# The last four chunks of one tile in seven products instead of eight, two loads on GpSimd's queue, and a start cut finer on TensorE

## Chip, cores, metric

The kernel runs on one core of a Trainium2 chip. Time is the device time of that core in microseconds (us). The engines are TensorE (PE, matrix products, with its weight loads PEld), VectorE (DVE), ScalarE (ACT), GpSimd (POOL) and SyncE (SP), which here only issues DMAs. An engine works through its own queue in order. A DMA is issued by an engine's queue and then moved by 16 DMA engines that all queues share.

## What is computed

Lightning attention in blocks with a decay for each head, and behind it a SwiGLU network. Cut to what matters (B = 4, H = 8, S = 768, D = 64; 3072 tokens, model dimension 512, inner dimension 1536):

```
for each block b of 64 positions:
    intra = (qb @ kb.T * Dmask) @ vb                  # Dmask: lam ** (i - j) for i >= j
    inter = (qb * lam_pow) @ kv_state
    out[b] = intra + inter
    kv_state = lam ** 64 * kv_state + (kb * rev_pow).T @ vb
x = out, heads side by side                           # 3072 x 512
g = x @ w_gate; v = x @ w_val                         # 512 x 1536 each
result = (g * sigmoid(g) * v) @ w_out                 # 1536 x 512
```

## The kernel before

**Tiles and groups.** The tokens are handled in six tiles t = 0..5 of 512 tokens. A tile is made of two groups of 256 tokens; group g (0 to 11) belongs to tile g // 2. For each group k, q and v are loaded (load_group, L263; load_fp32, L109), k is cast to bfloat16 by ScalarE and q scaled and cast by VectorE (cast_scaled, L277, its two instructions at L281 and L283), both are transposed by one DMA (dma_transpose, L268, tile qkt), and v is scaled by GpSimd into v_s (v_scale, L255). From group 6 on k and q are loaded in four DMAs each (L122), of 64 partitions and 128 KB.

**Attention of a group** has these pieces on TensorE: scores(g) (L376), masked by VectorE into ssb (L381); core_a(g), the product with the state (inter, L502); core_b(g), the product within the block (intra, L515), whose result ScalarE copies into the tile's input xt (evac, L527); upd_mm(g) (L408), the update of the state, copied out by ScalarE (upd_copy, L430) and added up by GpSimd (state, L463); the copies of the state for TensorE (kvn, L443, L445) stand in a list kvq and are issued by kv_flush. attend(g) (L863) runs core_a(g), then upd_mm, scores of g + 1, core_b(g) and state of g + 1.

**The network, two ways.** In tiles 0 to 3 each of the twelve chunks of 128 inner columns is a step: ffn_fc (L580) makes four gate products of 512 columns (L558), silu on ScalarE (L562), four value products (L574) and the multiplication into h on VectorE (L577). In tiles 4 and 5 ffn_unit(t, j) (L686) makes four chunks at once, 2j, 2j + 1 and the same of the second half, by a seven-product scheme: the model dimension and the inner dimension are each cut in two, and the tokens of a tile are split by blocks, so that a product of two 2 x 2 block matrices takes seven block products and not eight. Each of the seven is eight instructions of 256 columns at L703 (two matrices, two chunk columns, two parts of the model dimension). For it sums and differences of weights are made on VectorE (w_combo, L651, instruction L666: n = 0, 1, 2 into ws, n = 3 in place into the weights), and of the inputs (x_combo, L672, instruction L684; the fourth, n = 3, in place into xt). The unit copies and adds partial results with ScalarE (L737, L740) and VectorE (L745, L753), takes silu at L730 and multiplies at L733, three times on VectorE and once on GpSimd. The product with w_out is done in the same seven-product way in all tiles but tile 0 (out_units, L775, instruction L793), with combinations of w_out (wo_combo, L614) and of h (h_combo, L625, instruction L640).

**What sets the order.** Everything is written by hand: the kernel runs under a manual schedule, so each engine's instructions stand in the order in which the program makes them. `steps` is the list of chunks, `plan` says with at(step, fn, ...) what follows a step, and the loop at L1151 works it off. Small VectorE instructions (h_combo, and later x_combo, w_combo) stand in the list `trickle`, from which drip(n) takes n at places between products. Masks wait in `later` until run_later. PSUM has eight banks, handed out in a ring by bank(); a unit takes six fixed ones. SBUF tiles come from pools with few buffers: raw (10) for loads and combinations, qkt (3) for transposed q and k, h (5), ups (4), sil (3).

**Around the change.** Tile 3 is the loop of L1114 for t = 3: twelve chunks in the order 0, 1, 6, 7, 2, 3, 8, 9, 4, 5, 10, 11 (L1115), attend(8) after the sixth and attend(9) after the eleventh (AT, L1113), cast_scaled(9) and load_group(10) after the first, cast_scaled(10) and load_group(11) after the seventh (L1120 to L1122). WS (L1099) says after which step each w_combo comes; the lists from L1178 on gives what is dripped in out_units(2) (L1184). k of group 11 is loaded on ScalarE's queue (KACT, L325), all else on SP's. The kernel begins with TensorE products on constants (L179 to L184) that compute nothing.

Of the kernel before, what the change touches and what calls it, by code (L numbers as in the profile page):

```python
# [37 lines left out]
def _body(ctx, tc, nc, q, k, v, lam, moe_w_gate, moe_w_val, moe_w_out, out):  # L38
# [140 lines left out]
    for n in range(30):  # L179
        r = slice(n % 2 * 64, n % 2 * 64 + 64)  # L180
        nc.tensor.matmul(b[r, 0:8], warm[r, 0:64], warm[r, 0:8], start=True, stop=True, skip_group_check=True)
    warm_up(2)
    nc.tensor.matmul(lam_ps[:, 0:H], ones[:, 0:128], lam_row, start=True, stop=True)
    warm_up(4)  # L184
# [78 lines left out]
    def load_group(g, parts="kqv"):  # L263
        for src, what in ((k, "kraw"), (q, "qraw"), (v, "v")):
            if what[0] in parts:
                load_fp32(g, nc.scalar if what == "kraw" and g in KACT else nc.sync, src, what)

# [57 lines left out]
    KACT = (11,)  # L325
# [344 lines left out]
    XS0 = 4  # L670

    def x_combo(t, n, g):  # L672

        xt = st[("xt", t)]
        g = slice(0, 2) if g is None else slice(g, g + 1)
        b11, b12 = xt[:, g, 0:KH, 0], xt[:, g, 0:KH, 1]
        b21, b22 = xt[:, g, KH:MC, 0], xt[:, g, KH:MC, 1]
        if t not in xs:
            pool, tag = (qkt_pool, "qkt") if t == XS0 else (raw_pool, "raw")  # L680
            xs[t] = pool.tile([128, 3, 2, KH, BLK], BF16, name="xs", tag=tag)
        x = [xs[t][:, m, g] for m in range(3)]
        o, i0, i1 = ((x[0], b12, b11), (x[1], b22, x[0]), (x[2], b21, x[1]), (b12, b22, b12))[n]
        nc.vector.tensor_tensor(out=o, in0=i0, in1=i1, op=ALU.subtract)  # L684

    def ffn_unit(t, j, bk, early=None, mid=None, dr=(0, 0, 2)):  # L686
# [51 lines left out]
        for i in range(2):  # L738
            product(i, E[i], wa(0, 1), xb(0, 1), True)
            nc.scalar.copy(out=es[i], in_=E[i])  # L740
# [28 lines left out]
        h_combo(t, j)  # L769
# [328 lines left out]
    outs = []  # L1098
    WS = [(x, n, i, 0, 3) for x, n, i in ((110, 0, 0), (112, 0, 1), (206, 1, 0), (210, 1, 1), (301, 2, 0), (303, 2, 1))] + [(308, 3, 0, 0, 2), (309, 3, 1, 0, 2)]  # L1099
    XC = 8  # L1100
    D0 = (0, 0, 3)
# [8 lines left out]
    A9 = 10  # L1110
    C11 = None
    sns = {0: s1a, 1: s1b + s2h}
    AT = {2: (7, 10), 3: (A8, A9)}  # L1113
    for t in range(2, 4):  # L1114
        order = [c for j in range(FC // 4) for c in (2 * j, 2 * j + 1, FH + 2 * j, FH + 2 * j + 1)]  # L1115
# [4 lines left out]
        for j, g in ((4 if t == 2 else 0, 2 * t + 3), (8 if t == 2 else 6, 2 * t + 4)):  # L1120
            at(sn[j], cast_scaled, g)
            at(sn[j], load_group, g + 1)  # L1122
            if g > 7:
                at(sn[1 + j], v_scale, g, nc.gpsimd, 0, H // 2)
                at(sn[(1 if t == 2 else 2) + j], v_scale, g, nc.gpsimd, H // 2, H)
        for i in range(2):
            at(sn[AT[t][i]], attend, 2 * t + 2 + i)
        if t == 2:
# [6 lines left out]
            at(sn[9], h_combo, t, (0, 2))  # L1135
        else:
            at(sn[7], h_combo, t, (0, 2))
        at(sn[11], h_combo, t, 2)
    sn = sns[3]
    if C11 is not None:  # L1140
        at(sn[C11], cast_scaled, 11)
    XM = (1, 1)
    W3L = ()
# [3 lines left out]
    if not XM[0]:  # L1147
        for n in (0, 3, 1, 2):
            at(sn[XC], x_combo, 4, n, 0)

    for n, (t, fc, b0, b1) in enumerate(steps):  # L1151
# [6 lines left out]
        todo = plan.get(n, [])  # L1158
        busy = [f for f, x in todo if f in (attend, ahead, cast_scaled, v_scale)]
        if not busy:  # L1160
            drip(2 if len(trickle) > 4 else 1)
        for fn, *a in [(f, *x) for f, x in todo]:
            if fn is out_units:
                drip(sum(x[0] <= a[0] for x in trickle))
            fn(*a)
            if fn in (attend, ahead):
                run_later(1)
    run_later(len(later))
# [15 lines left out]
    out_units(2, many=list(M2))  # L1184
# [11 lines left out]
    trickle[:0] = [soon(w_combo, i, 3, (2, 3)) for i in range(2)]  # L1196
    def early():
        fixed[:] = [s0, s1]
        scores(11)

# [56 lines left out]
```

## Time and profile before

| | |
|---|---|
| runs | 217.79, 217.82, 219.28 us; median 217.82 |
| the profiled execution | 218.1 us |
| its span, first to last instruction | 216.3 us |
| instructions in it | 6883 |
| TensorE clock granted | 1.000 (mean) |
| HBM read, written | 28.31 MB, 6.29 MB |
| DMA on queue q1 (SP) | 38.22 MB |
| DMA on queue q10 (ACT) | 1.11 MB |

A row of the timeline reads: start in us, length in us, engine (with q: its queue), line, operation, what is written and read, count; in brackets the idle time just before and what ended it. A row of the chain of waits reads: start, length, engine, tile, line, count. A row of the stretches reads: stretch, its length, and for PE, PEld, DVE, ACT and POOL the busy time and the instructions, then the granted clock, the DMA share and GB/s. Ends of TensorE instructions are modelled, and a few of its records are missing from the trace.

### The profile page before, as it was taken

To read this page: it belongs to the slowest core of one execution; us is meant where nothing else is said; L and a number is where in the kernel's file an instruction comes from. 1 tells how busy PE (TensorE), PEld (TensorE's weight loads), DVE (VectorE), ACT (ScalarE), POOL (GpSimd) and SP (SyncE) were. 2 spreads that over 40 slices of the span, in tenths; PEclk is the share of its full clock that TensorE was granted. 3 is DMA by queue.
4 is the path that set the end of the run, shared out by engine and by line. 5 is a ranking of instruction groups with operands and counts; after the bars stand their busy time and mean duration, and the time that the engine had idled before them with its cause. 6 is when DMAs were issued, how large, how long until landed. Compare 5 with 4: busy or idle time off the path is not lost.

```text
span 216.3 us, 6883 instructions
## 1 busy us (share of the span) xinstructions
PE 209.8 (97%) x2813; PEld 153.3 (71%) x2816; DVE 149.5 (69%) x267; ACT 129.1 (60%) x280; POOL 92.3 (43%) x126
## 2 busy tenths in 40 slices
PE   8899999999999999999999999999999999999994
PEld 4666455888887447666754545888888888888883
DVE  1774447576677989775478988886797379961760
ACT  5788577666545254638368478754872766636522
POOL 6684755818498240685962336510740022200200
PEclk9999999999999999999999999999999999999999
DMA  6999999999999878999678899481000500005014
GB/s 189 346 354 345 378 337 321 290 249 232 315 352 151 191 214 190 257 186 238 168 169 236 203 230 215 103 225 68 2 5 3 194 0 3 0 3 194 0 52 146
DMA packets 88320, 39.76 MB, mean 184 GB/s; under 512 B 57698, under 2 KB 83938, under 8 KB 88290
## 3 DMA queue, kind: packets, MB, share of 16 engines
q1 hardware_dynamic: 84978, 38.22, 64.9%
q10 hardware_dynamic: 3312, 1.11, 2.0%
q8 instruction: 22, 0.36, 0.7%
q14 instruction: 8, 0.07, 0.1%
HBM read 28.31 MB, written 6.29 MB: 160 GB/s over the span
## 4 chain that ended last, share of the span: by engine, by line
PE 73%; DVE 7%; DMA 6%; SPq 5%; ACT 3%; issue 2%; POOL 2%; POOLq 1%; DVEq 0%
PE bank L793 20%; PE bank L703 15%; PE bank L558 13%; PE bank L574 13%; DMA woraw<-in_moe_w_out_dram 4%; PE bank L593 4%; SPq L122 2%; DMA qraw<-in_q_dram 2%; SPq L247 2%; DVE ws L666 2%; DVE h L577 1%; PE bank L515 1%; PE bank L146 1%; DVE wt L623 1%; PE bank L502 1%
## 5 line engine op out<-in xcount | busy, mean ns | idle before, releaser
L577 DVE TENSOR_TENSOR h<-sil,bank 128x256 bf16<-128x256 bf16 (+1 forms) x67 | 34.8, 531 | 26.3 <-PE bank L574 18.0
L558 PE MATMUL bank<-xt,wg_sb 128*128 128x256 bf16 (+1 forms) x268 | 52.5, 319 | 0.0
L574 PE MATMUL bank<-xt,wv_sb 128*128 128x256 bf16 (+1 forms) x268 | 52.4, 319 | 0.0
L562 ACT ACTIVATE sil<-bank 128x256 bf16<-128x256 f32 (+1 forms) x67 | 31.7, 479 | 23.7 <-PE bank L558 16.8
L574 PEld LDWEIGHTS <-wv_sb 128*128 128x128 bf16 x268 | 26.0, 98 | 15.8 <-DVE wv_sb L988 0.5
L558 PEld LDWEIGHTS <-wg_sb 128*128 128x128 bf16 x268 | 25.2, 98 | 13.8 <-DVE xt L527 0.2
L258 POOL TENSOR_TENSOR v_s<-v,dec 128x512 bf16<-128x512 f32 (+1 forms) x18 | 24.1, 1356 | 24.0 <-DMA v<-in_v_dram 16.0
L733 POOL TENSOR_TENSOR h<-sil,es 128x512 bf16<-128x512 bf16 x6 | 7.0, 1163 | 50.0 <-ACT sil L730 50.0
L793 PEld LDWEIGHTS <-h 128*128 128x128 bf16 x240 | 23.3, 98 | 3.4 <-issue 0.3
L793 PE MATMUL bank<-wo_sb,h 128*128 128x256 bf16 x180 | 21.6, 273 | 0.1
L793 PEld LDWEIGHTS <-hs 128*128 128x128 bf16 x180 | 17.6, 98 | 2.9
L357 DVE TENSOR_TENSOR ssb<-bank,causal 128x512 bf16<-128x512 f32 x24 | 15.4, 681 | 1.8 <-PE bank L350 1.8
L745 DVE TENSOR_TENSOR bank<-bank,es 128x512 f32<-128x512 f32 x12 | 7.8, 693 | 11.4 <-PE bank L703 10.1
L703 PEld LDWEIGHTS <-ws 128*128 128x128 bf16 x144 | 13.8, 97 | 2.3 <-issue 0.2
L793 PE MATMUL bank<-wt,hs 128*128 128x256 bf16 x120 | 15.0, 272 | 0.0
L730 ACT ACTIVATE sil<-bank 128x512 bf16<-128x512 f32 x18 | 10.7, 596 | 7.0 <-POOL h L733 4.6
L463 POOL TENSOR_TENSOR kvf<-kvs,ups 128x256 f32<-128x256 f32 x8 | 6.5, 813 | 19.1 <-ACT ups L430 19.1
L733 DVE TENSOR_TENSOR h<-sil,bank 128x512 bf16<-128x512 bf16 x18 | 12.2, 682 | 1.4 <-ACT sil L730 1.4
L703 PE MATMUL bank<-xs,ws 128*128 128x256 bf16 x96 | 12.8, 272 | 0.0
L527 ACT CAST xt<-bank 128x512 bf16<-128x512 f32 x19 | 11.6, 658 | 2.0 <-PE bank L515 1.5
L463 POOL TENSOR_TENSOR kvf<-kvf,ups 128x256 f32<-128x256 f32 x16 | 12.2, 763 | 0.9
L703 PE MATMUL bank<-xt,wg_sb 128*128 128x256 bf16 x72 | 10.8, 273 | 0.2 <-ACT ups L430 0.2
(119 smaller groups left out, 361.3 us busy)
## 6 DMA issues: line engine op xcount, KB each, us to landing
out_dram<-osb SPq DMA_DIRECT2D x22, 256.0 KB, 2.1
v<-in_v_dram SPq DMA_DIRECT2D x18, 256.0 KB, 4.5
woraw<-in_moe_w_out_dram SPq DMA_DIRECT2D x6, 512.0 KB, 7.6
qraw<-in_q_dram SPq DMA_DIRECT2D x24, 128.0 KB, 3.2
wraw<-in_moe_w_gate_dram SPq DMA_DIRECT2D x5, 512.0 KB, 7.2
wraw<-in_moe_w_val_dram SPq DMA_DIRECT2D x5, 512.0 KB, 6.9
kraw<-in_k_dram SPq DMA_DIRECT2D x20, 128.0 KB, 3.1
kraw<-in_k_dram SPq DMA_DIRECT2D x4, 512.0 KB, 6.6
```

The source lines that it names most:

```text
L258: eng.tensor_tensor(out=st[("vs", g)][:, h0:h1], in0=st[("v", g)][:, h0:h1].rearrange("p h (s d) -> p h s d", s=2), in1=vfac(g, h0, h1), o ...
L357: nc.vector.tensor_tensor(out=ssb[:, h2, 2 * c:2 * c + 2].rearrange("p a s n -> p a (s n)"), in0=sp[(c, h2)].rearrange("p (a x) -> p a x", ...
L463: nc.gpsimd.tensor_tensor(out=o, in0=f, in1=u, op=ALU.add)
L527: fns[r](out=xt[:, g % 2, :, r].rearrange("p h (m s) -> p h s m", s=2) if g < NAT0 else xt[:, g % 2, :, :, r * M:r * M + M], in_=op[r].rea ...
L558: nc.tensor.matmul(gp[:, 0:N], wg_sb[:, mc, fs], xt[:, b0 // 2:b1 // 2, mc].rearrange("p g b n -> p g (b n)"), start=(mc == 0), stop=(mc = ...
L562: nc.scalar.activation(sil[:, 0:N], gp[:, 0:N], AF.Silu)
L574: nc.tensor.matmul(vp[:, 0:N], wv_sb[:, mc, fs], xt[:, b0 // 2:b1 // 2, mc].rearrange("p g b n -> p g (b n)"), start=(mc == 0), stop=(mc = ...
L577: nc.vector.tensor_tensor(out=h_sb[:, fc % FH, b0:b1].rearrange("p b n -> p (b n)"), in0=sil[:, 0:N], in1=vp[:, 0:N], op=ALU.mult)
L703: nc.tensor.matmul(o[:, fi * 256:fi * 256 + 256], lhs(i, c, 2 * j + fi), rhs(c), start=(start and fi == 0 and c == 0), stop=(c == KH - 1), ...
L730: nc.scalar.activation(sil[key], src, AF.Silu)
L733: eng.tensor_tensor(out=h_of(half, r), in0=v3(sil[half, r]), in1=v3(src), op=ALU.mult)
L793: nc.tensor.matmul(o, lhs(f), rhs(f), start=(start and f == 0), stop=(f == FH - 1), skip_group_check=True)
```

## The change

It does four things. (1) The last four chunks of tile 3 (4, 5, 10, 11) leave the loop and are made by ffn_unit(3, 2) in a new function unit3; core_a(9) stands inside that unit, and upd_mm(10), scores(10), core_b(9) and state(10) behind it. For this x_combo runs for tile 3 as well, after chunk steps 3, 4, 6 and 7, and its fourth result goes into a tile of its own (in all tiles) and not into xt, since eight chunks of tile 3 still read xt as it was; all w_combo n = 0, 1, 2 are done by the end of tile 2, n = 3 for the columns of these four chunks after steps 0 and 5 of tile 3, and for the others in two halves in out_units(2). out_units(2) gets its banks from the unit. (2) k of groups 10 and 11 is loaded by GpSimd's queue; before, by SP's and ScalarE's. (3) At the start 33 small products stand in place of 30, and 24 products of 128 columns in place of 6 of 512. (4) h_combo of tiles 4 and 5 does the columns of units 0 and 1 at once after unit 1, and four VectorE instructions are dripped earlier in the first unit of tile 4 (E0, D0). By the built programs TensorE has 5721 instructions and had 5631, VectorE as many as before, ScalarE loses four DMAs and gains seven other instructions, SP loses four DMAs.

```diff
-    for n in range(30):
+    for n in range(33):
...
-    warm_up(2)
+    warm_up(8, 128)
     nc.tensor.matmul(lam_ps[:, 0:H], ones[:, 0:128], lam_row, start=True, stop=True)
-    warm_up(4)
+    warm_up(16, 128)
...
-                load_fp32(g, nc.scalar if what == "kraw" and g in KACT else nc.sync, src, what)
+                load_fp32(g, nc.sync if what != "kraw" else KQ.get(g, nc.sync), src, what)
...
-    KACT = (11,)
+    MH = 0
+    KQ = {10: nc.gpsimd, 11: nc.gpsimd}
...
-            pool, tag = (qkt_pool, "qkt") if t == XS0 else (raw_pool, "raw")
-            xs[t] = pool.tile([128, 3, 2, KH, BLK], BF16, name="xs", tag=tag)
-        x = [xs[t][:, m, g] for m in range(3)]
-        o, i0, i1 = ((x[0], b12, b11), (x[1], b22, x[0]), (x[2], b21, x[1]), (b12, b22, b12))[n]
+            pool, tag = (raw_pool, "raw") if t == 5 else (qkt_pool, "qkt")
+            xs[t] = pool.tile([128, 4, 2, KH, BLK], BF16, name="xs", tag=tag)
+        x = [xs[t][:, m, g] for m in range(4)]
+        o, i0, i1 = ((x[0], b12, b11), (x[1], b22, x[0]), (x[2], b21, x[1]), (x[3], b22, b12))[n]
...
         for i in range(2):
-            product(i, E[i], wa(0, 1), xb(0, 1), True)
+            product(i, E[i], wa(0, 1), xsum(3), True)
...
-        h_combo(t, j)
+        if t == 3 or j != MH:
+            h_combo(t, (0, 2) if t > 3 and MH == 0 and j == 1 else j)
...
+    def unit3():
+        bk = [(ring[0] + i) % 8 for i in range(6)]
+        ring[0] += 6
+        assert primed[bk[4]] == primed[bk[5]] == 512
+        ffn_unit(3, 2, bk, lambda: (drip(EU[0]), kv_flush()), lambda: (drip(EU[1]), core_a(9)), DU)
+        upd_mm(10)
+        upd_copy(10)
+        scores(10)
+        late, later[:] = later[:], []
+        core_b(9)
+        later[:] = late
+        state(10)
+        st["bk2"] = [bk[n] for n in (4, 0, 2, 5, 1, 3)]
+
-    WS = [(x, n, i, 0, 3) for x, n, i in ((110, 0, 0), (112, 0, 1), (206, 1, 0), (210, 1, 1), (301, 2, 0), (303, 2, 1))] + [(308, 3, 0, 0, 2), (309, 3, 1, 0, 2)]
-    XC = 8
-    D0 = (0, 0, 3)
+    WS = [(x, n, i, 0, 3) for x, n, i in ((110, 0, 0), (111, 0, 1), (206, 1, 0), (207, 1, 1), (210, 2, 0), (211, 2, 1))] + [(300, 3, 0, 2, 3), (305, 3, 1, 2, 3)]
+    DU = (0, 0, 2)
+    XT = (3, 4, 6, 7)
+    EU = (0, 0)
+    E0 = 4
+    D0 = (0,0,0)
...
-    A9 = 10
...
-    AT = {2: (7, 10), 3: (A8, A9)}
+    AT = {2: (7, 10), 3: (A8,)}
     for t in range(2, 4):
-        order = [c for j in range(FC // 4) for c in (2 * j, 2 * j + 1, FH + 2 * j, FH + 2 * j + 1)]
+        order = [c for j in range(FC // 4 - 1) for c in (2 * j, 2 * j + 1, FH + 2 * j, FH + 2 * j + 1)]
...
-                at(sn[(1 if t == 2 else 2) + j], v_scale, g, nc.gpsimd, H // 2, H)
-        for i in range(2):
-            at(sn[AT[t][i]], attend, 2 * t + 2 + i)
+                at(sn[1 + j], v_scale, g, nc.gpsimd, H // 2, H)
+        for i, x in enumerate(AT[t]):
+            at(sn[x], attend, 2 * t + 2 + i)
...
             at(sn[9], h_combo, t, (0, 2))
+            at(sn[11], h_combo, t, 2)
         else:
             at(sn[7], h_combo, t, (0, 2))
-        at(sn[11], h_combo, t, 2)
+            for n, x in enumerate(XT):
+                at(sn[x], x_combo, 3, (0, 3, 1, 2)[n], None)
...
-    W3L = ()
+    W3L = (0, 1)
...
         todo = plan.get(n, [])
+        front = [x for x in todo if x[0] is w_combo or x[0] is x_combo]
+        todo = [x for x in todo if x not in front] + front
...
     run_later(len(later))
+    unit3()
+    run_later(len(later))
     new_xt(5)
...
-    out_units(2, many=list(M2))
+    out_units(2, bk=st["bk2"], many=list(M2))
...
-    trickle[:0] = [soon(w_combo, i, 3, (2, 3)) for i in range(2)]
     def early():
         fixed[:] = [s0, s1]
         scores(11)
+        drip(E0)
```

## The prediction

> **What bounds the kernel now.** I read the page first, then the busy time by stretches, the chain of waits, and last the timelines of single engines around tile 3, where most of the change lies.
>
> ```profile
> PE 209.8 (97%) x2813; PEld 153.3 (71%) x2816; DVE 149.5 (69%) x267; ACT 129.1 (60%) x280; POOL 92.3 (43%) x126
> ...
> PE 73%; DVE 7%; DMA 6%; SPq 5%; ACT 3%; issue 2%; POOL 2%; POOLq 1%; DVEq 0%
> ```
>
> TensorE (PE) is busy for 97% of the span and holds 73% of the chain. A busy PE need not be a fast PE, so the second view asks for the stretches one by one (columns: PE, PEld, DVE, ACT, POOL busy, clock, DMA share).
>
> ```profile
> 110.20:122.40 12.20, 12.20 (x63) 5.40 (x61) 10.99 (x14) 8.35 (x17) 5.54 (x5) 1.00 0.84 207
> 123.80:135.70 11.90, 11.90 (x178) 5.97 (x171) 9.78 (x15) 9.52 (x21) 6.08 (x8) 1.00 0.98 220
> 169.50:188.20 18.70, 18.70 (x169) 16.29 (x167) 14.77 (x26) 12.76 (x24) 3.07 (x3) 1.00 0.11 42
> ```
>
> Tile 3 (the first two rows) has no idle PE, and DVE works 10.99 of 12.20 us in its first half: DVE is the engine with least room there. The third row is three seven-product units in a row, again with no idle PE. So what the change gives is read from PE's own instructions, and what it may lose from whether the others still keep pace.
>
> ```profile
> 126.59 0.86 PE bank L574 x4
> ...
> 132.63 0.38 PE bank L502 x32
> ...
> 169.45 18.80 PE bank L703 x168
> ```
>
> The chain of waits gives the prices: four 512-column products take 0.86 us (215 ns each), and 168 products of the units take 18.80 us (111.9 ns each, all the small delays inside a unit included).
>
> **The change part by part.**
>
> *Seven products.* Removed: chunks 4, 5, 10 and 11 of tile 3, each 4 gate and 4 value products: 4 x (0.86 + 0.86) = 6.88 us. Added: one unit, 7 products x 2 matrices x 2 chunk columns x 2 halves of the model dimension = 56 instructions of 256 columns: 56 x 0.1119 = 6.27 us. Net -0.61 us, all on PE, which is the path.
>
> *Attention of group 9 in pieces.* Before, core_a(9), upd_mm(10), scores(10) and core_b(9) stood together from 132.56 to 133.84. Now core_a(9) is inside the unit and the rest behind it, so PE changes twice more between 64x64 and 128x128 tiles. In the unit of tile 4 the same piece occupies 150.57 to 150.94, 0.37 us, against the 0.38 us of the row above, so the piece itself costs the same; such a change of form shows as about 0.1 us (the idle 0.42 us of the weight loads "issue" at 132.56 is mostly hidden). I take +0.1, with ends 0 and +0.3.
>
> *The unit's exit.* The next work behind the unit's last product is upd_mm(10), scores(10), core_b(9) (about 1.28 - 0.38 = 0.9 us), then out_units(2), whose first two products write the banks that the last silu and the last multiplication of the unit read.
>
> ```profile
> 151.51 1.17 POOL L733 TENSOR_TENSOR h<-sil,es 128x512 bf16<-128x512 bf16 x1 [10.20 <-ACT sil L730]
> ...
> 152.71 0.60 ACT L730 ACTIVATE sil<-bank 128x512 bf16<-128x512 f32 x1 [0.74 <-POOL h L733]
> ```
>
> In tile 4's unit the last silu waits 0.74 us for GpSimd's multiplication (it needs the buffer), and ends at 153.31, 1.37 us behind the last product's end (151.94). With 0.9 to 1.1 us of cover PE waits 0 to 0.45 us, and half of that may be had back because scores(10) waits for the bank of an earlier multiplication anyway. I take +0.1, ends 0 and +0.6.
>
> *DVE's work.* Four x_combo (0.41 us each by the undisturbed rows of L684) are new in tile 3, and two w_combo n=3 of a third of the width; w_combo n=1 and n=2 move up, the second of n=2 to ahead of tile 3, and two thirds of n=3 move behind the unit. From chunk 0 to 7 of tile 3 the balance is about +0.5 us on DVE. What covers it: the multiplications into h may lag by two steps of 1.73 us before a bank is missed; and the unit's third product, the first that needs x[1], starts 16 x 0.112 = 1.8 us behind the unit's start at 127.45, at 129.2. DVE in its new order, from the h of 122.44 on: three h 2.0, two masks 1.36, one h_combo, one w_combo and two x_combo 1.64, the cast of q 1.23, in all 6.2, so x[1] is there at 128.7. If that 0.5 us is gone, PE waits by the rest. One h_combo of 1024 columns (0.68) in place of two of 512 (0.42 each) in tiles 4 and 5 frees DVE 4 x 0.16 us a tile where PE does not wait: 0. Cost 0, ends -0.1 and +0.6.
>
> *k by GpSimd's queue.* Four DMAs of k leave SP for group 10 (2.69 us of its queue) and four leave ScalarE's queue for group 11 (2.8 us); q and v of both groups move up behind them, and GpSimd issues eight.
>
> ```profile
> 111.25 2.13 POOL L463 TENSOR_TENSOR kvf<-kvf,ups 128x256 f32<-128x256 f32 x2
> 117.39 2.77 POOL L258 TENSOR_TENSOR v_s<-v,dec 128x512 bf16<-128x512 f32 x2 [4.01 <-PE bank L574]
> ...
> 124.71 1.53 POOL L463 TENSOR_TENSOR kvf<-kvf,ups 128x256 f32<-128x256 f32 x2
> 130.11 2.41 POOL L258 TENSOR_TENSOR v_s<-v,dec 128x512 bf16<-128x512 f32 x2 [3.86 <-PE bank L558]
> ```
>
> The four DMAs of group 10 fall into GpSimd's gap 113.38 to 117.39, those of group 11 into 126.24 to 130.11. Behind them in the queue stand v_scale(9), wanted by upd_mm(9) at 122.62, v_scale(10), wanted at about 133.9, and the unit's L733 at about 133.6. So with d us an issue, nothing is late while 113.4 + 4d + 2.8 is below 122.6 (d below 1.6) and 126.2 + 4d + 2.6 is below 133.6 (d below 1.2). The trace of before has no DMA from GpSimd. Lower end: the same DMA on SP and ACT.
>
> ```profile
> 118.71 2.69 SPq L122 DMA_DIRECT2D kraw<-in_k_dram  x4
> ...
> 125.87 2.12 ACTq L122 DMA_DIRECT2D kraw<-in_k_dram  x3
> ```
>
> That is 0.67 and 0.71 us each. Upper end: GpSimd is held until the data land, 3.1 us by the issue table. I take 0.7, the nearest row, since it is the same operation: cost 0. At 3.1 it would be 13.6 us (rival 1). As the 512 KB of k for group 10 now go beside v of group 9, at some 210 GB/s v lands up to 2.4 us later, and v_scale(9) ends at 122.6 instead of 120.2: just in time; 0, with an end at +0.3.
>
> *The start.* Six products of 512 columns become 24 of 128: the same 3,072 columns, and at this stage 128-column instructions run at 0.43 / 4 = 108 ns against 0.427 us for 512. Three more small ones are 3 x 0.032 = 0.1 us, ahead of a product that waits for lam's landing. The 42 instructions also shift where PE runs dry:
>
> ```profile
> 13.88 0.41 PE L408 MATMUL bank<-v_s,qk 64*64 64x64 bf16 x28 [0.29 <-issue]
> ...
> 19.65 0.43 DVE L988 CAST wv_sb<-wraw 128x512 bf16<-128x512 f32 x1 [2.50 <-DMA wraw<-in_moe_w_val_dram]
> ...
> 20.13 0.33 PEld L574 LDWEIGHTS <-wv_sb 128*128 128x128 bf16 x3 [0.51 <-DVE wv_sb L988]
> ```
>
> At 13.88 PE stands still for about 0.5 us in a run of products with no wait in it. If that went, PE would only come earlier to 20.13, where it waits for weights whose cast waits for a DMA: 0. Ends -0.4 and +0.1.
>
> PE's clock is still low there: four transposes take 0.43 us at 5.12, against 1.04 us for sixteen at 31.53. If the added instructions raised it sooner, that too would end at 20.13.
>
> *Sum.* -0.61 + 0.1 + 0.1 = -0.41 us. The profiled execution took 218.1 us (span 216.3), so 217.7 for it; it stands 0.28 above the median of the runs, 217.82, so the median becomes 217.4.
>
> **The rivals.**
>
> 1. GpSimd's queue is slow (slower than before). The point is d = 1.2 us an issue. At d = 2, about midway between the ends: v_scale(9) ends at 113.4 + 8 + 2.8 = 124.2, 1.6 late; group 11 starts 1.6 later, and 126.2 + 1.6 + 8 + 2.6 = 138.4 against 135.2, 3.2 late: +4.8, 222.2 us. At 3.1: 6.0 and 7.6, 231 us. For it: each of these DMAs is cut into 512 pieces of 256 bytes (64 partitions by 8 heads), as the code's loads of group 6 and later do. Against it: on SP and ACT the pieces cost nothing extra that the rows show.
>
> 2. DVE keeps GpSimd from issuing. That the two get in each other's way is seen: L666 took 1.82 us at 117.42 beside v_scale, its twin 0.94 us at 121.57 with GpSimd idle. If GpSimd could issue only while DVE is idle, the four issues of group 10 (2.8 us) would find 1.2 us of it in 12.2 and take some 28 us: v_scale(9) 22 us late, 239 us. Against it: v_scale itself ran on at 2.77 us beside a busy DVE, against 2.41 at 130.11. The Trainium skill, "SBUF — State Buffer", SBUF: two separate sides, has this as a trap: descriptors of a GpSimd DMA are not written while DVE holds the shared port in a two-port mode; by that sentence this rival would come true. Its section Who interferes with whom takes two-input operations out of it, since they hold only the read side, and nearly all DVE work of tile 3 has two inputs; no trace here shows which holds.
>
> 3. The gain is used up at the unit's edges: x[1] 0.3 late, the exit 0.4. Then -0.61 + 0.1 + 0.7 = +0.2, 218.0 us. For it: DVE is 90% busy there. Against it: the units at 169.5 to 188.2 run with none of this.
>
> 4. More is gained: the stall at 13.88 goes and is not taken back at 20.13, and the edges cost nothing: -0.61 - 0.4, 216.8 us. Against it: the DMA-bound cast.
>
> **How the numbers follow.** The forecast 0.50, rival 1 0.14, rival 2 0.02, rival 3 0.20, rival 4 0.14. The forecast and rivals 3 and 4 lie within 1% (2.2 us, about what a measurement of this kernel tells from no change) and rivals 1 and 2 beyond it, but for a rival 1 that is just past its point. Faster by over 1% needs 215.6, which no term reaches: 0.04. Slower: 0.15, rest 0.81. Range 216.6 to 219.8: below it lies rival 4 with every cost at its lower end, above it rival 1 from d = 1.7 on (0.4 + 2.0 = 2.4 on top of 217.4), and rival 2.
>
> **What would show it.** Right: L703 has 56 more instructions in 6.3 us, ending about 0.4 us sooner against tile 3's first step; no PE idle behind v_s or h at upd_mm(10); GpSimd's DMA issues at or under 1.2 us. Wrong: PE waits for POOL v_s or POOL h (rivals 1 and 2, told apart by whether the issues are long only beside DVE's work), for DVE xs or the sil of L730 (rival 3), or passes the weights' cast of L988 sooner and keeps it (rival 4).

## The result, and the profile after

The changed kernel took 221.47 us (median of 6 runs, 219.66 to 222.07 for five of them, 224.16 for one) against 218.01 us of the kernel before (6 runs): ratio 1.0129, 95% interval 1.0089 to 1.0169. A ratio leaves out runs in a slower state, here the one of 224.16 us with a granted clock of 0.99, so it is below the quotient of the two medians. A second set (after_again, below) gave 1.0103 (1.0037 to 1.0169). Forecast were 217.4 us, a ratio of 0.998. The profiled execution took 222.07 us, span 220.0. From here on, lines of the changed kernel stand one higher than before from about L330 on (L408 is L409, L558 is L559, L640 is L641, L666 is L667, L793 is L794), but for L684 to L753, which keep their numbers.

The page of the changed kernel, busy time and the chain's shares by engine:

```profile
PE 210.1 (95%) x2861; PEld 157.5 (72%) x2861; DVE 152.1 (69%) x268; ACT 131.1 (60%) x284; POOL 99.0 (45%) x135
...
PE 63%; DMA 19%; SPq 9%; DVE 2%; issue 2%; ACT 2%; POOL 1%; POOLq 1%; DVEq 0%; ACTq 0%
```

TensorE is busy as long as before, in a span 3.7 us longer: the time went into idle TensorE. DMA's share of the chain rose from 6 to 19%. The stretches of tile 3 and of three later units (same columns as before):

```profile
111.50:123.70 12.20, 12.20 (x64) 5.41 (x60) 11.82 (x18) 8.19 (x17) 7.94 (x9) 1.00 0.94 240
124.90:138.20 13.30, 11.54 (x194) 8.10 (x193) 12.44 (x19) 10.59 (x23) 8.66 (x11) 1.00 1.00 157
173.20:191.90 18.70, 18.70 (x169) 16.32 (x168) 14.11 (x24) 12.68 (x24) 3.16 (x3) 1.00 0.11 40
```

The later units are as they were. In the second half of tile 3 TensorE is idle for 1.76 us (13.30 - 11.54), and VectorE is busy for 11.82 us of 12.20 in the first half. The timelines show what TensorE waited for (GpSimd, VectorE and TensorE in this order):

```profile
114.54 2.90 POOL L122 DMA_DIRECT2D kraw<-in_k_dram  x4
117.82 2.27 POOL L258 TENSOR_TENSOR v_s<-v,dec 128x512 bf16<-128x512 f32 x2 [0.37 <-PE bank L559]
...
127.58 2.72 POOL L122 DMA_DIRECT2D kraw<-in_k_dram  x4
130.31 2.06 POOL L258 TENSOR_TENSOR v_s<-v,dec 128x512 bf16<-128x512 f32 x2
```

```profile
130.15 2.52 DVE L684 TENSOR_TENSOR xs<-xt,xs 128x512 bf16<-128x512 bf16 x1
```

```profile
133.33 1.20 PE L703 MATMUL bank<-xs,ws 128*128 128x256 bf16 x8 [1.34 <-DVE bank L745]
```

GpSimd's DMAs take 0.68 to 0.73 us each on average over four, and both v_scale are in time. But x_combo n = 2 takes 2.52 us in place of 0.41: it ends 0.3 us behind v_scale(10). L745 stands behind it on VectorE, and TensorE waits 1.34 us inside the unit. The chain of waits shows the rest of tile 3:

```profile
129.44 8.05 DMA qkt<-qk
...
137.53 0.45 PE bank L377 x32
137.98 0.29 PE bank L516 x30
138.27 1.09 PE bank L794 x9
139.36 0.81 issue
140.17 8.35 PE bank L794 x75
```

The DMA transpose of group 10 needs 8.05 us (4.0 before), and scores(10) waits 0.41 us for it; then TensorE stops for 0.81 us at the tenth product of out_units(2), with nothing in the profile that it waits for. And the start:

```profile
13.99 0.26 PE L409 MATMUL bank<-v_s,qk 64*64 64x64 bf16 x8 [0.45 <-POOL v_s L258]
14.99 0.38 PE L409 MATMUL bank<-v_s,qk 64*64 64x64 bf16 x24 [0.75 <-POOL v_s L258]
```

```profile
19.74 0.43 DVE L989 CAST wv_sb<-wraw 128x512 bf16<-128x512 f32 x1 [1.51 <-DMA wraw<-in_moe_w_val_dram]
```

upd_mm(1) waits for v_s of group 1 until 14.99, 1.1 us later than it went on before (13.88). The cast of wv, the wait that was to take up any shift here, is over at 20.17 and TensorE needs it at 21.03: no wait is left that could take the delay back.

Measured from the traces, in us. The marks between the stretches are the first products of the first chunk, of tile 3, of out_units(2) and of the unit after it:

| kernel | first chunk at | to tile 3 | tile 3 to out_units(2) | its unit, core_a(9) in it | out_units(2) |
|---|---|---|---|---|---|
| before | 15.13 | 96.79 | 23.66 | - | 9.17 |
| changed | 16.21 | 97.02 | 24.97 | 8.35 | 10.16 |
| changed, second execution | 15.84 | 96.44 | 24.54 | 8.35 | 10.65 |

From the first product of the first unit of tile 4 to that of the last out_units every kernel takes 58.6 us. So the changed kernel lost 1.08 us before the first chunk, 1.31 in tile 3 and 0.99 in out_units(2), the rest (0.35 us) in between and at the end.

### The profile page after: what moved, and what is told of

The parts are those of the page before. It is cut to its first block, busy times and chain, and to the rows that moved or that the text cites. A ratio compares the mean times of both kernels' runs of the same rounds, so it can differ in the third digit from the quotient of the medians.

```text
span 220.0 us, 6995 instructions
## 1 busy us (share of the span) xinstructions
PE 210.1 (95%) x2861; PEld 157.5 (72%) x2861; DVE 152.1 (69%) x268; ACT 131.1 (60%) x284; POOL 99.0 (45%) x135
## 3 DMA queue, kind: packets, MB, share of 16 engines
q0 software_dynamic: 384, 1.05, 1.9%
## 4 chain that ended last, share of the span: by engine, by line
PE 63%; DMA 19%; SPq 9%; DVE 2%; issue 2%; ACT 2%; POOL 1%; POOLq 1%; DVEq 0%; ACTq 0%
PE bank L794 19%; PE bank L703 15%; PE bank L559 10%; PE bank L575 9%; DMA qkt<-qk 7%; DMA qraw<-in_q_dram 6%; PE bank L594 5%; SPq L115 3%; SPq L233 3%; DMA v<-in_v_dram 3%; DMA wraw<-in_moe_w_val_dram 3%; SPq L122 2%; PE bank L516 1%; PE bank L503 1%; PE bank L377 1%
## 5 line engine op out<-in xcount | busy, mean ns | idle before, releaser
L578 DVE TENSOR_TENSOR h<-sil,bank 128x256 bf16<-128x256 bf16 (+1 forms) x63 | 32.1, 523 | 24.0 <-PE bank L575 17.9
L559 PE MATMUL bank<-xt,wg_sb 128*128 128x256 bf16 (+1 forms) x252 | 48.4, 315 | 0.0
L575 PE MATMUL bank<-xt,wv_sb 128*128 128x256 bf16 (+1 forms) x252 | 48.3, 315 | 0.0
L563 ACT ACTIVATE sil<-bank 128x256 bf16<-128x256 f32 (+1 forms) x63 | 29.6, 474 | 23.2 <-PE bank L559 18.0
L575 PEld LDWEIGHTS <-wv_sb 128*128 128x128 bf16 x252 | 24.6, 98 | 13.6
L559 PEld LDWEIGHTS <-wg_sb 128*128 128x128 bf16 x252 | 23.7, 98 | 12.0 <-DVE xt L528 0.2
L733 POOL TENSOR_TENSOR h<-sil,es 128x512 bf16<-128x512 bf16 x7 | 8.1, 1163 | 53.5 <-ACT sil L730 53.0
L258 POOL TENSOR_TENSOR v_s<-v,dec 128x512 bf16<-128x512 f32 (+1 forms) x18 | 22.2, 1252 | 16.8 <-DMA v<-in_v_dram 16.5
L794 PEld LDWEIGHTS <-h 128*128 128x128 bf16 x240 | 23.2, 98 | 4.2 <-issue 1.3
L794 PE MATMUL bank<-wo_sb,h 128*128 128x256 bf16 x180 | 21.8, 273 | 0.9 <-issue 0.8
L794 PEld LDWEIGHTS <-hs 128*128 128x128 bf16 x180 | 17.6, 98 | 3.2 <-issue 0.3
L703 PEld LDWEIGHTS <-ws 128*128 128x128 bf16 x168 | 16.0, 97 | 4.2 <-issue 1.9
L730 ACT ACTIVATE sil<-bank 128x512 bf16<-128x512 f32 x21 | 12.5, 595 | 7.9 <-POOL h L733 5.5
L745 DVE TENSOR_TENSOR bank<-bank,es 128x512 f32<-128x512 f32 x14 | 9.1, 693 | 11.2 <-PE bank L703 8.7
L703 PE MATMUL bank<-xs,ws 128*128 128x256 bf16 x112 | 15.1, 272 | 1.3 <-DVE bank L745 1.3
L733 DVE TENSOR_TENSOR h<-sil,bank 128x512 bf16<-128x512 bf16 x21 | 14.2, 683 | 2.8 <-ACT sil L730 2.8
L794 PE MATMUL bank<-wt,hs 128*128 128x256 bf16 x120 | 15.0, 272 | 0.1
L703 PEld LDWEIGHTS <-wg_sb 128*128 128x128 bf16 x112 | 10.9, 98 | 1.8 <-issue 0.3
```

Source lines behind the costliest of these rows:

```text
L258: eng.tensor_tensor(out=st[("vs", g)][:, h0:h1], in0=st[("v", g)][:, h0:h1].rearrange("p h (s d) -> p h s d", s=2), in1=vfac(g, h0, h1), o ...
L559: nc.tensor.matmul(gp[:, 0:N], wg_sb[:, mc, fs], xt[:, b0 // 2:b1 // 2, mc].rearrange("p g b n -> p g (b n)"), start=(mc == 0), stop=(mc = ...
L563: nc.scalar.activation(sil[:, 0:N], gp[:, 0:N], AF.Silu)
L575: nc.tensor.matmul(vp[:, 0:N], wv_sb[:, mc, fs], xt[:, b0 // 2:b1 // 2, mc].rearrange("p g b n -> p g (b n)"), start=(mc == 0), stop=(mc = ...
L578: nc.vector.tensor_tensor(out=h_sb[:, fc % FH, b0:b1].rearrange("p b n -> p (b n)"), in0=sil[:, 0:N], in1=vp[:, 0:N], op=ALU.mult)
L703: nc.tensor.matmul(o[:, fi * 256:fi * 256 + 256], lhs(i, c, 2 * j + fi), rhs(c), start=(start and fi == 0 and c == 0), stop=(c == KH - 1), ...
```

## The experiments

Each was timed together with the kernel before on the same chip, and has its ratio to it with the 95% interval; 1% is 2.2 us. The rows are those of one profiled execution of each.

### The parts of the change

**after_again**: the changed kernel once more, in a set of its own.

> The changed kernel as it is, on the same chip as its parts. If the 8.05 us of the transpose of group 10 and the 2.52 us of x_combo n = 2 belong to the kernel, both are seen again and it takes 221.2 us (1.0129 of the kernel before). If they were chance of the one profiled execution, the transpose takes 4.5 to 6.2 us, x_combo n = 2 under 1 us, and the profiled execution is near 220.5 us.

Ratio 1.0103 (1.0037 to 1.0169); profiled 221.18 us. The hold of x_combo n = 2 (VectorE) and the stop in out_units(2) (TensorE) were seen again:

```profile
129.20 2.52 DVE L684 TENSOR_TENSOR xs<-xt,xs 128x512 bf16<-128x512 bf16 x1
```

```profile
139.29 1.80 PE L794 MATMUL bank<-wo_sb,h 128*128 128x256 bf16 x15 [1.31 <-issue]
```

The transpose took 7.6 us. So the hold, the slow transpose and the stop in out_units(2) stand in both profiled executions and are not the chance of one.

**start_alone**: the kernel before, with the finer start.

```diff
-    for n in range(30):
+    for n in range(33):
-    warm_up(2)
+    warm_up(8, 128)
-    warm_up(4)
+    warm_up(16, 128)
```

> The former kernel with only the finer start (33 small products, 8 and 16 products of 128 columns). Theory A (the start costs about 1 us by a later v of group 1): 219.0 us against 218.0, and upd_mm(1) waits for POOL v_s. Theory B (chance, or made up later): 218.0 us, within 0.2 us.

Ratio 1.0059 (1.0024 to 1.0093): theory A, 1.3 us. The timeline, and the landing of v's DMAs in the first 9 us (of the kernel before: 4.6/4.7/4.8):

```profile
14.82 0.38 PE L408 MATMUL bank<-v_s,qk 64*64 64x64 bf16 x24 [0.75 <-POOL v_s L258]
```

```profile
DMA to landing us min/median/max: 4.6/5.3/5.8
```

A DMA reports its landing in sixteen steps, as many as there are DMA engines. Read from the trace for the two DMAs of v of group 1, with the first fetch of instructions for TensorE (queue q8, one packet of 16 KB, 0.93 to 0.96 us long), in us:

```
               fetch at   v, first half: 15 steps by / last   v, second half: 15 steps by / last
before         11.52      11.30 / 11.33                       12.11 / 12.15
start_alone    10.07      11.62 / 12.64                       12.40 / 13.27
changed        10.26      11.60 / 12.82                       12.42 / 13.47
```

Fifteen steps come within about 0.3 us of when they did; the last is 1.1 to 1.5 us late. 42 more instructions ahead bring TensorE's fetch 1.3 to 1.5 us forward, into the time when v is still being moved. That it holds one DMA engine which still has v to move is how I read this: the trace does not say which engine a packet ran on, but one step alone is late, by about the length of the fetch's packet. All seventeen traces divide by the time of this fetch: where it came at 9.3 to 11.43 us (eleven), the last step of the second half came at 13.1 to 13.6; where it came at 11.52 to 12.36 (six), at 12.04 to 12.39. With the finer start it came early, and v late, in all eight traces. The former start stands on both sides: of seven traces five had v in time and two had it late (gpsimd_alone, fetch at 11.38, and sums_old_start, at 11.22). So the finer start makes a delay constant that the former one has in some executions.

**old_start**: the changed kernel with the former start (the diff above the other way round).

> The changed kernel with the former start on TensorE (30 small products, 2 and 4 products of 512 columns); all else as changed. Theory A (the finer start costs about 1 us: with it v of group 1 lands about 1 us later, and upd_mm(1) waits 0.75 us for v_s at 14.99): TensorE passes upd_mm(1) about 1 us sooner, and the kernel takes about 220.5 us against the 221.5 us of the changed one. Theory B (that landing is chance from one execution to the next, or is made up at the next wait for a DMA): 221.5 us, with upd_mm(1) early or late as it falls.

Ratio 1.0041 (1.0011 to 1.0070), 219.15 us: 0.6 to 0.9% below the changed kernel, theory A again. But the difference is not the start's alone: with everything shifted, the profiled execution had neither the long hold (x_combo n = 2 took 0.93 us) nor the slow transpose (4.67 us). start_alone is the cleaner price, and by it the start is about half of the loss.

**gpsimd_alone**: the kernel before with only k of groups 10 and 11 on GpSimd's queue.

```diff
-    load_fp32(g, nc.scalar if what == "kraw" and g in KACT else nc.sync, src, what)
+    load_fp32(g, nc.gpsimd if what == "kraw" and g in KACT else nc.sync, src, what)
...
-    KACT = (11,)
+    KACT = (10, 11)
```

> The former kernel with only k of groups 10 and 11 on GpSimd's queue. Theory Q (the loads by GpSimd are what costs): each issue 0.7 us, the transposes of group 10 take some 8 us and scores(10) waits for them, up to 4 us; 219 us or more. Theory U (the loads are harmless where no unit stands in tile 3): scores(10) without a wait, 218.0 us within 0.3.

Ratio 0.9975 (0.9947 to 1.0004): no loss, theory U. The transposes took 5.9 and 4.7 us, not 8, and TensorE has no wait for them.

**old_queues**: the changed kernel with the former queues for k.

```diff
-    KQ = {10: nc.gpsimd, 11: nc.gpsimd}
+    KQ = {11: nc.scalar}
```

> The changed kernel with k of group 10 on SP's queue and k of group 11 on ScalarE's, as it was; unit and start as changed. Theory Q (GpSimd's loads cost the time in tile 3: they hold v_scale(10) until 130.31, so that it runs beside x_combo n = 2, which took 2.52 us in place of 0.41 and made TensorE wait 1.34 us for L745; and the DMA transpose of group 10 took 8.05 us, for 0.41 us of waiting at scores(10)): x_combo n = 2 takes 0.41 us, the transpose some 4 to 5 us, TensorE's idle time of 2.6 us between 131 and 141 is down to under 0.8 us, and the kernel takes 219.0 to 219.7 us. Theory U (the unit itself costs it: in its order x_combo n = 2 and v_scale(10) fall together whatever queue loads k): x_combo n = 2 still takes over 2 us, and the kernel takes 221 us or more.

Ratio 1.0035 (0.9999 to 1.0071), 219.54 us. Theory Q holds as to the rows: x_combo n = 2 takes 0.42 us, the transposes 3.7 to 4.0, no stop in out_units(2). But tile 3 still took 24.32 us, with two waits of another kind:

```profile
PE bank L377 <- DVE h L733: 0.4, 1, 0.4
PE bank L703 <- ACT bank L737: 0.4, 1, 0.4
```

**unit_alone**: both undone, the seven products alone.

> The changed kernel with the former start and k of groups 10 and 11 on SP's and ScalarE's queue: only the seven products and what they move are left of the change. Theory 1 (the unit gives what was forecast for it, about 0.4 us; the loss is the start's 1.3 us, as measured alone, and something that GpSimd's loads do to the unit): 217.7 to 218.0 us, ratio 0.997 to 0.999. Theory 2 (the unit itself loses at its edges and GpSimd's loads are as harmless as they were in the former kernel): 219.0 us or more, ratio 1.003 to 1.007, as with GpSimd's loads (old_start, 1.0041).

Ratio 1.0002 (0.9968 to 1.0036), between the two theories: no gain of the unit by itself is to be seen, and no loss. Tile 3 took 24.28 us, the unit 7.36. ScalarE's queue and TensorE:

```profile
126.36 2.44 ACTq L122 DMA_DIRECT2D kraw<-in_k_dram  x3
128.90 0.60 ACT L563 ACTIVATE sil<-bank 128x512 bf16<-128x512 f32 x1 [1.81 <-PE bank L703]
129.40 1.08 ACT L737 COPY bank<-bank 128x512 f32<-128x512 f32 x2
```

```profile
130.04 1.08 PE L703 MATMUL bank<-xs,ws 128*128 128x256 bf16 x8 [0.37 <-ACT bank L737]
...
136.02 0.44 PE L377 MATMUL bank<-qkt 64*64 64x64 bf16 x30 [0.43 <-DVE h L733]
```

ScalarE issues k of group 11 just ahead of the last silu of the eight chunks; that one and L737 come late, and with them the unit.

### The start: is it the fetch?

**same_count**: the finer cut with as many instructions as before.

```diff
-    for n in range(30):
+    for n in range(12):
-    warm_up(2)
+    warm_up(8, 128)
-    warm_up(4)
+    warm_up(16, 128)
```

> The former kernel with the finer start's 24 products of 128 columns, but 12 small products in place of 33, so that as many instructions stand ahead of the first transposes as before. Theory I (42 more instructions bring TensorE's next fetch of instructions forward, from 11.5 to 10.1 us, onto the DMA engine that still moves v of group 1, whose last sixteenth then lands at 13.3 in place of 12.2): with the old count the fetch starts at 11.0 us or later, v of group 1 lands by 12.4, and the kernel takes 218.3 us, within 0.4. Theory W (it is the finer cut as such, by the clock or the weight loads): 219.6 us, as with the whole finer start (start_alone, 1.0059).

Ratio 1.0001 (0.9958 to 1.0045): theory I as to the time, though not as to the landing of v in the profiled execution. The twelve runs fall in two groups, six of 217.92 to 218.39 us and six of 218.9 to 220.9; in the profiled one, of the upper group, the fetch came at 11.43 and the second half of v at 13.45.

**fewer_small**: the kernel before with 12 small products for 30, 36 instructions fewer.

> The former kernel with 12 small products in place of 30 at its start, 36 instructions fewer ahead of the first transposes. Theory I: the fetch of instructions starts at about 12.5 us, behind the landing of v of group 1, upd_mm(1) never waits for v_s, and the kernel takes 217.8 to 218.3 us. Theory W (the fetch does not matter): 218.3 us too, but v of group 1 late as often as in the former kernel; or slower, if TensorE starts on the transposes at a lower clock.

Ratio 1.0050 (1.0019 to 1.0082): slower, and theory I missed the time. v is in time (12.04, fetch at 12.36), as it said. Theory W allowed a slower kernel if TensorE's clock stayed low for longer; the trace's first record of the full clock comes at 7.24 us, within the 5.47 to 8.01 us of the sixteen others (7.66 in gpsimd_alone, which lost nothing). Now it is the instructions that come late, the kernel's own rows:

```profile
14.58 0.28 PE L408 MATMUL bank<-v_s,qk 64*64 64x64 bf16 x10 [0.82 <-issue]
```

```profile
53.23 0.25 PE L515 MATMUL bank<-ssb,v_s 64*64 64x128 bf16 x4 [1.11 <-issue]
```

By TensorE's list of instructions in the built programs these stops stand at instructions 447 and 1471. Such stops with "issue" in other kernels stand at 447 too (13.88 in the kernel before), at 1983 (1.79 us in same_count) and at 4031 (the changed kernel's tenth product of out_units(2), both executions): always 447 plus a multiple of 256, one fetch of 16 KB. In each TensorE went on 1.26 to 1.62 us behind the end of that fetch's packet. So a fetch too early goes with a late v, and one too late stops TensorE; the kernel before has it at 11.52, on the edge between.

### Tile 3: who holds whom

**x2_early**: the changed kernel with x_combo n = 2 right behind n = 1.

```diff
-    XT = (3, 4, 6, 7)
+    XT = (3, 4, 6, 6)
```

> The changed kernel with x_combo n = 2 of tile 3 right behind n = 1, one multiplication into h earlier on VectorE, so that it is over before GpSimd begins v_scale(10); nothing else moves. Theory L (VectorE and GpSimd shut each other out, and what jams between 131 and 137 us, k of group 11 and the transpose of group 10, hangs on the same meeting): x_combo n = 2 takes 0.42 us and not 2.52, TensorE no longer waits 1.34 us for L745, the transpose takes 4.5 to 5 us and TensorE does not stop in out_units(2): 219.3 us, ratio 1.004 as in old_start. Theory J (two things: the wait for L745 comes from the meeting, the jam from the fourth DMA of k and the transpose being issued within 0.2 us of each other): the 1.34 us go, but the transpose still takes 7 to 8 us and TensorE still stops about 1 us at the ninth product of out_units(2): 220.0 us, ratio 1.007.

Ratio 1.0104 (1.0045 to 1.0162), a miss of both theories: now the pair was caught (VectorE, then TensorE's waits).

```profile
129.57 3.38 DVE L684 TENSOR_TENSOR xs<-xt,xs 128x512 bf16<-128x512 bf16 x2
```

```profile
PE bank L703 <- DVE xs L684: 2.0, 1, 2.0
```

The first of them began inside GpSimd's fourth DMA (129.44 to 130.13) and ended 0.29 us behind the v_scale(10) that followed (132.20). At its usual 0.41 us it would have been over 0.15 us before v_scale(10) began, so overlap by the undisturbed lengths does not tell which sum is caught. But the transpose took 4.5 us and TensorE did not stop in out_units(2): the meeting and the jam are two things, and theory L falls.

**k11_scalar**: `KQ = {10: nc.gpsimd, 11: nc.scalar}` in the changed kernel.

> The changed kernel with k of group 11 back on ScalarE's queue, k of group 10 by GpSimd as changed. GpSimd then issues nothing ahead of v_scale(10), and the transpose of group 10 has no DMA of GpSimd beside it. Theories L and J both say: x_combo n = 2 not held for both of v_scale's instructions (under 1 us), the transpose 4 to 5 us, 219.3 us, ratio 1.004. Rival: it is k of group 10 that costs (the transpose of group 9 late, v_scale(9) later): 221 us, ratio 1.011.

Ratio 1.0102 (1.0059 to 1.0144), a miss as to time. The transpose took 4.5 us and x_combo n = 2 1.01 us, as expected; but ScalarE's issues bring back the two waits of unit_alone (0.47 and 0.38 us) on top of the start. The rival's time (1.011) nearly came out, but not its mechanism: TensorE waits neither for the transpose of group 9 nor for v_scale(9).

**k11_later**: GpSimd issues k of group 11 behind v_scale(10).

```diff
-            at(sn[j], load_group, g + 1)
+            at(sn[j], load_group, g + 1, "qv" if g == 10 else "kqv")
...
                 at(sn[1 + j], v_scale, g, nc.gpsimd, H // 2, H)
+                if g == 10:
+                    at(sn[1 + j], load_group, 11, "k")
```

> The changed kernel with GpSimd's four DMAs of k of group 11 behind v_scale(10) in its queue and not ahead of it. Theory J: the transpose of group 10 is half done when they are issued; it takes 4 to 5.5 us, TensorE does not stop in out_units(2); v_scale(10) starts when v lands, about 129.2, and x_combo n = 2 is held for its second half at most, under 1.2 us: 219.5 us, ratio 1.005. Theory L: as J. Rival (any load by GpSimd beside a transpose slows it to 7 us or more): scores(10) waits 0.4 us or more for the transpose, TensorE stops in out_units(2), 220.5 us, ratio 1.010.

Ratio 1.0056 (1.0025 to 1.0087), as theory J says. The transpose took 3.7 us, the unit 6.69 and tile 3 23.16, less than forecast; but the price is paid in out_units(2) (11.07 us):

```profile
129.30 0.42 DVE L684 TENSOR_TENSOR xs<-xt,xs 128x512 bf16<-128x512 bf16 x1
```

```profile
PE bank L794 <- DVE h L733: 1.7, 1, 1.7
```

GpSimd's multiplication L733 now stands behind the DMAs (134.32), and h_combo on VectorE meets it: L641 took 1.82 us there, and the last multiplication of the unit stood behind it.

**k11_last**: the former start, and GpSimd's DMAs behind L733.

```diff
         ffn_unit(3, 2, bk, lambda: (drip(EU[0]), kv_flush()), lambda: (drip(EU[1]), core_a(9)), DU)
+        load_group(11, "k")
```

> The changed kernel put together from what the other runs favour: the former start, the seven products, k of group 10 by GpSimd as changed, and GpSimd's four DMAs of k of group 11 only behind the unit's multiplication L733, so that neither v_scale(10) nor L733 stands behind them. If the three places named so far (the start's fetch of instructions, VectorE shut out behind GpSimd's last DMA, the jam of that DMA and the transpose) are all that the change lost, the stretch from tile 3's first step to out_units(2) takes 23.0 to 23.4 us (23.66 before, 24.97 as changed), out_units(2) 9.2 us, and the kernel 217.8 us, ratio 0.997 to 0.999. If the unit's own edges cost as well whatever GpSimd does (as in unit_alone, 24.28 us), that stretch takes 24 us or more and the kernel 218.7 us, ratio 1.001 to 1.003.

Ratio 1.0108 (1.0062 to 1.0154), a miss of both. The waits of TensorE:

```profile
PE bank L377 <- DVE h L578: 1.0, 1, 1.0
...
PE bank L794 <- DVE bank L819: 0.8, 1, 0.8
PE bank L575 <- DVE h L578: 0.5, 1, 0.5
```

Two h_combo met v_scale(9) (118.57 and 120.05, each 0.85 us over its usual time), which the edit does not touch, and VectorE fell behind; later the cast of k waited 2.47 us for its late load, and L819 behind it.

**sums_earlier**: x_combo n = 1 and n = 2 each a step earlier in the changed kernel, so that neither can meet v_scale(10); **sums_old_start** and **sums_old_queues**: the same with the former start, and with former start and queues.

```diff
-    XT = (3, 4, 6, 7)
+    XT = (3, 4, 5, 6)
```

> The changed kernel with x_combo n = 1 of tile 3 after its sixth step in place of its seventh and n = 2 after its seventh in place of its eighth; nothing else moves. If the meeting of x_combo n = 2 with v_scale(10) costs the 1.34 us: no sum is held for 2 us, TensorE does not wait for L745, the stretch from tile 3's first step to out_units(2) takes 23.2 to 23.6 us (24.97 and 24.54 as changed). If the jam of k of group 11 and the transpose of group 10 comes from their order and not from the meeting, TensorE may still stop 0.8 to 1.3 us in out_units(2). Time 219.4 us without the jam (ratio 1.004), 220.3 with it (1.008). If the edges cost by themselves: stretch over 24 us, ratio 1.009 or more.

Ratio 1.0054 (1.0019 to 1.0089): the meeting's share is gone, and what is left is as much as the start costs alone. VectorE and TensorE's waits after 118 us:

```profile
131.48 0.42 DVE L684 TENSOR_TENSOR xs<-xt,xs 128x512 bf16<-128x512 bf16 x1
131.81 0.68 DVE L578 TENSOR_TENSOR h<-sil,bank 128x512 bf16<-128x512 bf16 x1
132.85 1.30 DVE L745 TENSOR_TENSOR bank<-bank,es 128x512 f32<-128x512 f32 x2 [0.36 <-PE bank L703]
```

```profile
PE bank L377 <- DMA qkt<-qk: 0.5, 1, 0.5
```

L745 now waits for TensorE and not the other way. The unit took 6.69 us, tile 3 23.53, out_units(2) 9.18. The profiled execution took more than the median (221.58 us), for another reason: from the first chunk to tile 3 it needs 2.6 us more than the kernel before, 1.01 and 0.76 us of them in waits for VectorE (L819, L823).

> The same with the former start on TensorE: seven products, both k by GpSimd, sums a step earlier. If the start and the meeting are the two causes: the stretch 23.2 to 23.6 us, 217.8 us, ratio 0.998. If the edges cost by themselves: ratio 1.003 or more.

Ratio 1.0004 (0.9969 to 1.0038), tile 3 23.73 us: no loss, but not the gain that was expected. The unit took 6.69 us again, and scores(10) waited 0.83 us for the transpose; the chain of waits:

```profile
129.25 6.81 DMA qkt<-qk
136.05 0.04 issue
136.09 0.45 PE bank L377 x32
```

> The same with the former start and k of both groups on SP's and ScalarE's queue: only the seven products are left of the change. In unit_alone TensorE waited 0.37 us for ScalarE's L737, behind its four DMA issues, and 0.43 us for L733 at scores(10), and no sum met v_scale(10); if those two edges are what eats the unit's gain, they stay and the stretch takes 24.2 us, ratio 1.000. If VectorE's order was behind them, it takes 23.5 us, ratio 0.997.

Ratio 1.0063 (1.0029 to 1.0097). The stretch took 24.48 us, with 0.60 us of waiting for ScalarE's L737 and 0.44 for L733: the two edges stay, as the first theory says. Its ratio (1.000) was too low, and why is open: the kernel differs from unit_alone only in the two sums, its profiled span is the same within 0.1 us (217.5), and yet the ratio is 0.6% higher. Differences of that size between two kernels of this list are therefore not safe to read by the ratio alone.

**The jam** (the slow transpose of group 10). Beside GpSimd's DMAs the transpose of group 10 took, by the time from the start of GpSimd's fourth DMA of k to its own: -0.18 us (it was ahead) 8.05 and 7.6 us; -0.09, 6.8; +0.22 to +0.43 behind it, 4.7, 4.5, 4.7 and once 6.3 (its last step alone late, a fetch beside it). With k of group 11 on ScalarE's queue it took 3.8 to 4.5. That it goes with the order is seen in seven traces; why is open, and no run changed the order alone.

## Why the prediction was wrong, point by point

Three places failed: the start and DVE's work, which the sum has at 0, and out_units(2), for which it has no term. The seven products, the first term, were right.

- **The seven products** were sized right. Where nothing met, the unit with core_a(9) took 6.69 us in three kernels (sums_earlier, sums_old_start, k11_later); 6.27 + 0.37 were forecast.
- **The start, "0. Ends -0.4 and +0.1"**: mis-sized, and the wrong way. It cost 1.3 us (start_alone, 1.0059). The step read the stall at 13.88 as something that shifts and then ends at 20.13 behind the cast of wv. Moved instructions also move the fetch, here to a time when v was still landing (the step came 1.3 us late; that both used one DMA engine is argued, not recorded); and at 20.13 there were only 0.51 us of waiting, which cannot take up a whole microsecond.
- **DVE's work, "Cost 0, ends -0.1 and +0.6"**: failed in the step "0.41 us each by the undisturbed rows of L684", and in looking at x[1] alone. x[2] (x_combo n = 2) was held 2.1 us, and TensorE waited 1.34 us for L745 behind it. Rival 2 had named the row that shows it, L666 at 117.42 with 1.82 us beside v_scale, and used it only for GpSimd's issues. Without the meeting the kernel is 0.5 to 0.75% faster (sums_earlier against the changed kernel's 1.0103 and 1.0129).
- The Trainium skill, "SBUF — State Buffer", Who interferes with whom, says that a VectorE instruction with two inputs in SBUF contends with a GpSimd instruction that reads SBUF; by its section SBUF: two separate sides whichever of the two starts first gets the shared pair of ports for the whole instruction. The traces agree with the first half: the sums held here (L684, L641, L667) have both inputs in SBUF, v_scale reads SBUF, and masks and multiplications with an input in PSUM were not held. They bear out the second in part. In k11_later x_combo n = 2 began 0.02 us ahead of v_scale(10) and took 0.42 us, and the first instruction of v_scale took 1.30 us in place of 1.05; in unit_alone the two began about 0.01 us apart and took 0.42 and 1.34. But in the changed kernel x_combo n = 2 began 0.16 us ahead and was held through both instructions of v_scale. The three long holds (the changed kernel twice, x2_early) all began while GpSimd was issuing its fourth DMA; other sums began during an issue and were not held (129.21 in the changed kernel, 131.48 in sums_earlier), so why is open. The prediction drew on these sections for the descriptors only, and the exception for two-input operations that rival 2 named agrees with the trace: the issues kept to 0.7 us beside a busy VectorE.
- **k by GpSimd's queue, d = 0.7**: right (0.68 to 0.73), so rivals 1 and 2 fell, and alone it costs nothing (gpsimd_alone). What the step left out is what stands beside those DMAs: the transpose at 4.5 to 8.05 us, and v_scale(10) right behind the last of them.
- **The unit's exit and edges, +0.2**: too small without GpSimd's queue: the stretch was 1.2 us over 23.66 - 0.61 in unit_alone, two waits of 0.4 us being the part that the rows name. Rival 3 (x[1] late, the exit 0.4) had about the size of it, but not the place: ScalarE's four issues ahead of the unit. Moving k of group 11 away from ScalarE took that edge away and put the meeting with VectorE in its place.
- **out_units(2)**, not a step of the prediction at all: its 0.8 to 1.3 us are a late fetch again. The 42 instructions of the start move the boundary at 4031 from about the 31st product of out_units(2), where it lies with the former start and the unit, to the tenth, right behind 96 short products that use instructions up fast. Five other kernels have it there without such a stop. Here the fetch started just when the jammed transpose had landed (137.65 after 137.49; 136.52 after 136.11); that it waited for the transpose is likely but not shown, and in sums_earlier it started 2.1 us ahead of the landing.

So the 1.0 to 1.3% are about 0.6% of the start (start_alone) and about 0.5 to 0.75% of the meeting and the jam (sums_earlier), each known to some 0.4% at best. No kernel tried shows the 0.6 us of the seven products in its time; in unit_alone 0.80 us of waits at the unit's edges take them up. None of the kernels tried is shown to be faster than the one before; the closest is gpsimd_alone.

## What to carry to other kernels

Price a moved VectorE instruction with two SBUF inputs by its row beside a GpSimd instruction that reads SBUF, not by its undisturbed row, and ask of every one of them what GpSimd runs at that moment. Adding instructions that compute nothing need not be free on an engine whose instructions are fetched by DMA: find the "issue" stalls, see whether they stand 256 instructions apart, and look at which loads are landing when the fetch moves. A wait downstream takes up a delay only as far as the idle time it shows.

## What the runs showed of the hardware that was not expected

- TensorE's instructions come in fetches of 16 KB for 256 instructions (22 packets of queue q8 in each trace, 0.88 to 1.87 us long). In the eleven traces where the first fetch started by 11.43 us, the last of the sixteen steps of v's DMA came about 1 us late; and a late fetch stops TensorE for 0.3 to 1.8 us, at instruction 447 or a multiple of 256 behind it.
- Four DMAs of 128 KB by GpSimd's queue are issued in 2.72 to 2.90 us, about as fast as by SP's (2.69), but move in larger packets: 384 packets for 1.05 MB, against 1200 for 0.59 MB on ScalarE's queue.
- A held VectorE instruction ended 0.28 to 0.30 us behind the end of a v_scale in the changed kernel (both executions), x2_early and old_start.
- From the start of the last unit's last product to the end, kernels with DMAs by GpSimd took 13.13 to 13.35 us, those without 13.01 to 13.03; why is open.
